# Two more blocks of the down projection by Strassen, gelu tiles moved into the weight memory, and a new order in the last group of a GeGLU kernel

## The chip, the cores and the metric

The kernel runs on one core of one Trainium2 chip. The metric is device time in microseconds (us), as the median of several executions. Each was compared with executions of the kernel before on the same chip, in the same rounds. The engines are named as in the profile: PE is TensorE (matmuls), PEld its weight loads, DVE VectorE, ACT ScalarE, POOL GpSimd, SP SyncE.

## The reference

```python
B, S, D, F = 1, 2048, 1024, 3584          # all bf16

def reference(x, w_gate, w_up, w_down):
    return (_gelu(x @ w_gate) * (x @ w_up)) @ w_down
```

## The kernel before

The tokens are worked off in two halves (h), each in two stages. The up stage makes hT = gelu(gate) * up, two blocks of 128 of F at a time. The down stage multiplies hT (28 blocks of 128 along F) by w_down, in two groups (grp) of 512 tokens. In both stages PE is relieved by Strassen's scheme: seven products (m1 to m7) instead of eight, at the price of sums of the operands, made by DVE, POOL and ACT in fp32 (t1 to t4 are sums of w_down, s1 to s4 sums of hT; a22 and b22 are copies). A "row" below is one tile of such a sum: 128 by 512 elements of w_down, 128 by 256 of hT. In down, 20 of the 28 blocks go this way (NS = 10 pairs of blocks). The other 8 are multiplied plainly, in NKK = 4 steps of 2 blocks.

Each engine takes its instructions strictly in program order: the helpers `dve`, `pool`, `act` chain them.

```python
def t_down(name, i0, i1):                  # sums of w_down, rows i0..i1 of 512
    ...
    if name in ("t2", "t4"):               # made earlier, read back from DRAM
        sp(nc.sync.dma_start(out=t.bitcast(F32), in_=src))
    elif name == "b22":
        act(nc.scalar.copy(out=t, in_=b(1, 1)))
    else:                                  # t1 and t3: on VectorE
        dve(nc.vector.tensor_tensor(out=t, in0=in0, in1=in1, op=ALU.subtract))

def s_down(hT, grp, name, i0, i1):         # sums of hT
    ...
    if name in ("s1", "s3"):
        pool(nc.gpsimd.tensor_tensor(out=t, in0=in0, in1=in1, op=op))
    else:                                  # s2 and s4
        dve(nc.vector.tensor_tensor(out=t, in0=in0, in1=in1, op=op))

def next_group():
    for i in range(0, NS, 2):
        s_down(hT, 1, "s1", i, i + 2)
    for i in range(0, NS, 2):
        s_down(hT, 1, "s3", i, i + 2)

def next_t(name, step):
    return [lambda i=i: t_down(name, i, i + step) for i in range(0, NS, step)]

then0 = {                                  # what group 0 queues behind its products
    "m5": next_t("t3", 5),
    "m4": next_t("t3", 5) + next_t("t1", 5) + [next_group],
}
```

After m4, a group runs its plain steps and evicts its eight PSUM banks. In program order this stands behind what `then0["m4"]` queued:

```python
on_act = b % 2 == (1 if last_grp else 0)
if on_act:
    act(nc.scalar.copy(out=dst, in_=banks[b][:]))
else:
    dve(nc.vector.tensor_copy(out=dst, in_=banks[b][:]))
```

So DVE makes the next group's t3 and t1 first and evicts banks 1, 3, 5 and 7 afterwards. The next group's m1 writes banks 0 and 1.

## Time and profile before

The median was 552.27 us.

| | before |
|---|---|
| PE busy | 541.3 of 550.5 us (98%) |
| DVE busy, whole span | 293.3 us (53%) |
| DVE busy in group 0 of the first half | 40.1 of 45.7 us |
| longest wait of PE | 0.9 us, in the start-up |
| pace of the up stage | 12.60 us a pair of blocks |

How to read it: PE is the bound, so another engine costs something only where PE waits for it. The average of DVE says nothing on that. Its 88% in group 0 does. The lines themselves stand in the prediction. One more from the list of transfers, since it answers to a later one: the last write of the output was the only one of these issued by ACT (size of each, and median us from issue to landing).

```profile
out_dram<-o_sb SPq DMA_DIRECT2D x7, 128.0 KB, 1.8
out_dram<-o_sb ACTq DMA_DIRECT2D x1, 128.0 KB, 2.6
```

### The profile page before, as it was taken

Reading aid. Unit: us, or ns where it says so; the run is one execution under the profiler, and the core shown is the slowest. Engines: PE = TensorE matmul, PEld = TensorE weight load, DVE = VectorE, ACT = ScalarE, POOL = GpSimd, SP = SyncE. Lnnn points to the kernel's source line nnn. Section 1 sums busy time; section 2 is a strip of 40 time slices with the busy share of each in tenths; the row PEclk is TensorE's granted clock in tenths of the full one; section 3 lists DMA queues with packets and bytes.
Section 4 is the critical chain, followed back from the end, with each engine's and each line's share of the span. In section 5 each row is a group of like instructions: output and inputs, shape, how many; then the busy total and the mean of one; then the engine's idle time right before and its main releaser. Section 6 shows DMA issues by size and latency. Waiting matters only on the chain.

```text
span 550.5 us, 7066 instructions
## 1 busy us (share of the span) xinstructions
PE 541.3 (98%) x2396; PEld 361.8 (66%) x2441; DVE 293.3 (53%) x355; ACT 245.1 (45%) x426; POOL 320.2 (58%) x248
## 2 busy tenths in 40 slices
PE   8999999999999999999999999999999999999996
PEld 3456777776777667467567767776677775765662
DVE  1714566655665896823644444444444449695402
ACT  2435545555555315117155555555555551502331
POOL 0487777777666804900598766777767763095000
PEclk9999999999999999999999999999999999999999
DMA  9642364462628789589932240405040527617803
GB/s 272 187 140 89 98 210 160 146 219 87 229 79 296 271 279 194 163 287 270 339 119 84 70 144 8 154 0 155 0 154 28 202 83 260 231 38 231 314 29 115
DMA packets 67363, 88.54 MB, mean 161 GB/s; under 512 B 15616, under 2 KB 46336, under 8 KB 67328
## 3 DMA queue, kind: packets, MB, share of 16 engines
q1 hardware_dynamic: 66640, 87.44, 49.4%
q10 hardware_dynamic: 688, 0.66, 0.4%
q8 instruction: 20, 0.33, 0.3%
q14 instruction: 15, 0.12, 0.1%
HBM read 75.50 MB, written 9.44 MB: 154 GB/s over the span
## 4 chain that ended last, share of the span: by engine, by line
PE 96%; DMA 2%; issue 0%; ACT 0%; ACTq 0%
PE bank L366 59%; PE bank L568 32%; PE bank L234 5%; DMA w_mem<-in_w_up_dram 1%; DMA wd_sb<-in_w_down_dram 1%; PE bank L288 0%; ACT o_sb L705 0%; ACTq L157 0%
## 5 line engine op out<-in xcount | busy, mean ns | idle before, releaser
L366 PE MATMUL bank<-t_mem,s_mem 128*128 128x512 f32 x1040 | 255.2, 399 | 0.0
L366 PEld LDWEIGHTS bank<-t_mem,s_mem 128*128 128x128 f32 x1040 | 195.4, 188 | 45.3
L340 POOL TENSOR_TENSOR s_mem<-w_mem 128x512 fp32r<-128x512 bf16 x104 | 125.1, 1222 | 129.1 <-PE bank L366 77.4
L389 DVE TENSOR_TENSOR bank<-bank,m 128x512 f32<-128x512 f32 x104 | 72.8, 700 | 103.3 <-ACT bank L409 91.6
L249 DVE TENSOR_TENSOR hT<-g_sb,bank 128x512 bf16<-128x512 f32 x112 | 76.8, 687 | 65.0 <-ACT g_sb L244 31.2
L244 ACT ACTIVATE g_sb<-bank 128x512 f32<-128x512 f32 x112 | 66.6, 597 | 87.4 <-DVE bank L389 49.9
L366 PE MATMUL bank<-xT,w_mem 128*128 128x512 bf16 x392 | 97.7, 380 | 1.3
L545 POOL TENSOR_TENSOR s_mem<-hT 128x512 fp32r<-128x512 bf16 (+1 forms) x32 | 67.5, 2140 | 53.2 <-PE bank L568 44.7
L568 PE MATMUL bank<-t_mem,s_mem 128*128 128x512 f32 x400 | 96.2, 397 | 0.1
L568 PEld LDWEIGHTS bank<-t_mem,s_mem 128*128 128x128 f32 x400 | 74.8, 188 | 18.1 <-issue 0.9
L568 PEld LDWEIGHTS <-hT 128*128 128x128 bf16 x416 | 39.5, 98 | 50.0 <-issue 4.4
L366 PEld LDWEIGHTS <-w_mem 128*128 128x128 bf16 x416 | 36.7, 98 | 50.5 <-issue 13.3
L495 DVE TENSOR_TENSOR t_mem<-w_mem 128x1024 fp32r<-128x1024 bf16 (+2 forms) x28 | 61.3, 2232 | 5.4 <-ACT s_mem L536 5.0
L340 POOL TENSOR_TENSOR s_mem<-s_mem,w_mem 128x512 fp32r<-128x512 f32 x52 | 61.1, 1194 | 0.0
L340 POOL TENSOR_TENSOR s_mem<-w_mem,s_mem 128x512 fp32r<-128x512 bf16 x52 | 60.0, 1173 | 0.0
L568 PE MATMUL bank<-wd_sb,hT 128*128 128x512 bf16 x244 | 55.1, 379 | 1.2 <-DMA wd_sb<-in_w_down_dram 0.4
L353 ACT CAST s_mem<-w_mem 128x512 fp32r<-128x512 bf16 x52 | 31.9, 615 | 34.0 <-PE bank L366 29.2
L404 ACT COPY m<-bank 128x512 f32<-128x512 f32 x52 | 30.6, 588 | 17.7 <-PE bank L366 17.7
L409 ACT COPY bank<-bank 128x512 f32<-128x512 f32 x52 | 29.6, 570 | 17.0 <-PE bank L366 17.0
L400 ACT COPY bank<-bank 128x512 f32<-128x512 f32 x52 | 29.6, 570 | 14.2 <-PE bank L366 14.2
L568 PE MATMUL bank<-w_mem,hT 128*128 128x512 bf16 x154 | 35.6, 379 | 0.3
L705 ACT CAST o_sb<-bank 128x512 bf16<-128x512 f32 x16 | 9.4, 586 | 56.6 <-PE bank L568 56.6
(31 smaller groups left out, 196.2 us busy)
## 6 DMA issues: line engine op xcount, KB each, us to landing
t_mem<-t_dram SPq DMA_DIRECT2D x40, 512.0 KB, 5.1
w_mem<-in_w_gate_dram SPq DMA_DIRECT2D x11, 1024.0 KB, 5.5
w_mem<-in_w_up_dram SPq DMA_DIRECT2D x11, 1024.0 KB, 7.8
w_mem<-in_w_down_dram SPq DMA_DIRECT2D x10, 1024.0 KB, 7.9
wd_sb<-in_w_down_dram SPq DMA_DIRECT2D x16, 512.0 KB, 3.7
wd_sb<-in_w_down_dram SPq DMA_DIRECT2D x20, 256.0 KB, 7.0
t_dram<-o_sb SPq DMA_DIRECT2D x20, 256.0 KB, 2.0
out_dram<-o_sb SPq DMA_DIRECT2D x12, 256.0 KB, 2.4
```

The costliest lines, as they stand in the source:

```text
L244: act(nc.scalar.activation(out=g_sb[:], in_=ps[:], func=ACT.Gelu_apprx_tanh))
L249: nc.vector.tensor_tensor(out=hT[:, fc, tb * TB : (tb + 1) * TB], in0=g_sb[:], in1=ps[:], op=ALU.mult,)
L340: pool(nc.gpsimd.tensor_tensor(out=t, in0=in0, in1=in1, op=op))
L353: act(nc.scalar.copy(out=t, in_=a(1, 1)))
L366: nc.tensor.matmul(banks[bank][:], lhsT=lhs[:, c, :], rhs=rhs[:, c, :], start=start and c == 0, stop=c == KH - 1, skip_group_check=True,)
L389: nc.vector.tensor_tensor(out=banks[dst][:], in0=banks[src][:], in1=m5[j][:], op=ALU.add)
L400: act(nc.scalar.copy(out=banks[QB[j]][:], in_=banks[PB[j]][:]))
L404: act(nc.scalar.copy(out=m5[j][:], in_=banks[VB[j]][:]))
L409: act(nc.scalar.copy(out=banks[RB[j]][:], in_=banks[QB[j]][:]))
L495: dve(nc.vector.tensor_tensor(out=t, in0=in0, in1=in1, op=ALU.subtract))
L545: pool(nc.gpsimd.tensor_tensor(out=t, in0=in0, in1=in1, op=op))
L568: nc.tensor.matmul(banks[bank][:], lhsT=lhs, rhs=rhs, start=start, stop=stop, skip_group_check=True,)
```

## The change

The intent: one more pair of blocks by Strassen (NS = 11) saves PE two matmuls a group. To make room in SBUF, the gelu tiles get no pool of their own any more: they lie in a part of the shared weight memory that is free during the up stage. With three plain steps left, all three plain tiles fit their buffers, and the last group can finish bank by bank. The diff is cut: left out are larger t_mem and s_mem, the new addresses and times of the loads of w_down and of the plain tiles, the sums of the first half's t2 and t4 made one pair earlier, and pieces that end at NS where NS is odd.

```diff
-    NS = 10
+    NS = 11
...
-    g_pool = ctx.enter_context(tc.tile_pool(name="g", bufs=4))
...
     def gelu(ps):
-        g_sb = g_pool.tile([P, TB], F32, name="g_sb")
+        e0 = 4 * CH + (g_ctr[0] % 4) * 2 * TB
+        g_sb = w_mem[:, e0 : e0 + 2 * TB].bitcast(F32)
...
     def t_down(name, i0, i1):
-        if i0 < K2A < i1:
+        for cut in (16 - NS, 8):           # rows of w_down now lie in three places
+            if i0 < cut < i1:
+                t_down(name, i0, cut)
+                t_down(name, cut, i1)
+                return
...
         if last_grp:
-            steps[-2:] = [
-                [(NKK - 2, b) for b in VB + QB[:1]]
-                + [(NKK - 1, b) for b in PB + VB + QB[:1]]
-                + [(kk, b) for b in QB[1:] + RB for kk in (NKK - 2, NKK - 1)]
-            ]
+            steps = [[(kk, b) for b in OB for kk in range(NKK) if (kk, b) not in early]]
...                                        # the last write: SyncE instead of ScalarE
-                    if b == OB[-1]:
-                        nc.scalar.dma_start(...)
+                    sp(nc.sync.dma_start(...))
...                                        # last pair of the up stage
                     "m7": [
-                        lambda: s_down(hT, 0, "s1", 8, 10),
-                        lambda: s_down(hT, 0, "s3", 0, 2),
+                        lambda: s_down(hT, 0, "s1", 8, 11),
+                        lambda: s_down(hT, 0, "s3", 0, 1),
                         lambda: t_down("t1", 0, 2),
                         lambda: t_down("t1", 2, 4),
                     ],
                     "m3": [
-                        lambda: s_down(hT, 0, "s3", 2, 6),
+                        lambda: s_down(hT, 0, "s3", 1, 5),
                         lambda: t_down("t1", 4, 6),
                     ],
...                                        # "m4": s3 in 5..8 and 8..11, t1 in 6..8 and 8..11
```

With NS = 11, `next_t(..., 5)` and the cuts make four pieces of each t: 5, 3, 2 and 1 rows. Before it was three: 2, 3 and 5.

More of the change, by code (lines that the diff above doesn't have):

```diff
@@ L71 @@
     NWD = NH * NGRP * NKK
-    K2A = 12 - NS
     assert NTB == 2 and KF % 4 == 0 and NDN == 2 and TSB == 4 and NGRP == 2
-    assert (KF // FPG) % 2 == 1 and NS == 10
+    assert (KF // FPG) % 2 == 1 and NS == 11
     xv = x2.rearrange("t (ko ki) -> t ko ki", ki=P)
@@ L94 @@
     )
-    t_mem = shared_pool.tile([P, 5 * KH * TB], F32R, name="t_mem")
-    s_mem = shared_pool.tile([P, 10 * KH * P], F32R, name="s_mem")
-    w_mem = shared_pool.tile([P, 4 * KD * FG + 4 * KD * P], BF16, name="w_mem")
+    t_mem = shared_pool.tile([P, max(5 * KH * TB, 2 * NS * DN)], F32R, name="t_mem")
+    s_mem = shared_pool.tile([P, max(10 * KH * P, 4 * NS * P)], F32R, name="s_mem")
+    CH = KD * FG
+    w_mem = shared_pool.tile([P, 4 * CH + (2 * NS - 16) * D], BF16, name="w_mem")
     t_dram = dram_pool.tile([P, 2, NS, DN], F32, name="t_dram")
@@ L138, in pe @@
         return on("pe", inst)
-    CH = KD * FG
     xs0 = w_mem[:, 4 * CH : 4 * CH + TSB * D].rearrange("p (a b) -> p a b", b=D)
@@ L240, in mm_gu @@
         )
+    g_ctr = [0]
     def gelu(ps):
-        g_sb = g_pool.tile([P, TB], F32, name="g_sb")
-        act(nc.scalar.activation(out=g_sb[:], in_=ps[:], func=ACT.Gelu_apprx_tanh))
+        e0 = 4 * CH + (g_ctr[0] % 4) * 2 * TB
+        g_ctr[0] += 1
+        g_sb = w_mem[:, e0 : e0 + 2 * TB].bitcast(F32)
+        act(nc.scalar.activation(out=g_sb, in_=ps[:], func=ACT.Gelu_apprx_tanh))
         return g_sb
@@ L250, in mult @@
                 out=hT[:, fc, tb * TB : (tb + 1) * TB],
-                in0=g_sb[:],
+                in0=g_sb,
                 in1=ps[:],
@@ L453, in wd_rows @@
     def wd_rows(k0, k1):
-        e0 = 2 * CH + k0 * D if k1 <= NS + K2A else (k0 - NS - K2A) * D
+        assert k0 // 8 == (k1 - 1) // 8 or k0 >= 16
+        e0 = (2 * CH, 0, 4 * CH)[min(k0 // 8, 2)] + (k0 - 8 * min(k0 // 8, 2)) * D
         return w_mem[:, e0 : e0 + (k1 - k0) * D].rearrange("p (a b) -> p a b", b=D)
@@ L476, in t_down @@
     def t_down(name, i0, i1):
-        if i0 < K2A < i1:
-            t_down(name, i0, K2A)
-            t_down(name, K2A, i1)
-            return
+        for cut in (16 - NS, 8):
[3 more added lines that the diff above has]
+                return
         n = 0 if name in ("t1", "t2", "t4") else 1
@@ L610, in two, with g @@
         def two(f):
-            return lambda i: f(i - 1, i + 1) if i % 2 == 1 else None
+            def g(i):
+                if i % 2 == 1 or i == NS - 1:
+                    f(i - i % 2, i + 1)
+            return g
         def to_s2_t2(i0, i1):
@@ L629, in down_group @@
         base = (h * NGRP + grp) * NKK
-        load_wd_to(base + 3)
         product("m1", PB, h_block(0, 0), wd_block(0, 0), True)
@@ L638, in down_group @@
             act(nc.scalar.copy(out=m5[u][:], in_=banks[VB[u]][:]))
+        load_wd_to(base + 3)
         product("m2", PB, h_block(0, 1), wd_block(1, 0))
@@ L654, in down_group @@
         for i in range(0, NS, 2):
-            s_down(hT, grp, "a22", i, i + 2)
+            s_down(hT, grp, "a22", i, min(i + 2, NS))
         where = {}
@@ L708, in down_group @@
                 if last_grp:
-                    if b == OB[-1]:
-                        nc.scalar.dma_start(
-                            out=out2[r0 : r0 + P, c0 : c0 + DN], in_=dst
-                        )
-                    else:
-                        sp(
-                            nc.sync.dma_start(
-                                out=out2[r0 : r0 + P, c0 : c0 + DN], in_=dst
-                            )
-                        )
+                    sp(
+                        nc.sync.dma_start(out=out2[r0 : r0 + P, c0 : c0 + DN], in_=dst)
+                    )
                 elif whole:
@@ L742 @@
             first_pair = PPG
+            stage_load(0)
         for pair in range(first_pair, NPAIR):
@@ L751 @@
                 i = pair - first_pair
+                if i + 1 < NS:
+                    then["m2"] = [lambda i=i: stage_load(i + 1)]
                 if i < NS:
-                    then["m2"] = [lambda i=i: stage_load(i)]
-                if 1 <= i <= NS:
-                    then["m4"] = [lambda i=i: stage_sums(i - 1)]
+                    then["m4"] = [lambda i=i: stage_sums(i)]
             if pair == NPAIR - PPG:
-                for k0 in range(0, NS + K2A, 4):
+                for k0 in range(0, 8, 4):
                     load_wd_rows(k0, k0 + 4)
@@ L764 @@
                     "m2": [
-                        lambda: load_wd_rows(NS + K2A, NS + K2A + 4),
-                        lambda: load_wd_rows(NS + K2A + 4, 2 * NS),
-                        lambda h=h: load_wd_to(h * NGRP * NKK + 3),
+                        lambda: load_wd_rows(8, 12),
+                        lambda: load_wd_rows(12, 16),
                     ],
                     "m7": [
-                        lambda: s_down(hT, 0, "s1", 8, 10),
-                        lambda: s_down(hT, 0, "s3", 0, 2),
+                        lambda: s_down(hT, 0, "s1", 8, 11),
+                        lambda: s_down(hT, 0, "s3", 0, 1),
                         lambda: t_down("t1", 0, 2),
@@ L779 @@
                     "m4": [
-                        lambda: s_down(hT, 0, "s3", 6, 10),
+                        lambda: load_wd_rows(16, 19),
+                        lambda: load_wd_rows(19, 22),
+                        lambda: s_down(hT, 0, "s3", 5, 8),
+                        lambda: s_down(hT, 0, "s3", 8, 11),
                         lambda: t_down("t1", 6, 8),
-                        lambda: t_down("t1", 8, 10),
+                        lambda: t_down("t1", 8, 11),
                     ],
@@ L790, in next_group @@
             for i in range(0, NS, 2):
-                s_down(hT, 1, "s1", i, i + 2)
+                s_down(hT, 1, "s1", i, min(i + 2, NS))
             for i in range(0, NS, 2):
-                s_down(hT, 1, "s3", i, i + 2)
+                s_down(hT, 1, "s3", i, min(i + 2, NS))
         def next_t(name, step):
-            return [lambda i=i: t_down(name, i, i + step) for i in range(0, NS, step)]
+            return [
+                lambda i=i: t_down(name, i, min(i + step, NS))
+                for i in range(0, NS, step)
+            ]
         then0 = {
```

## The prediction

> **What bounds the kernel now.** I read the page first (busy shares, slices, chain), then the stretches of the four groups of the down projection, then the timeline engine by engine where one group hands over to the next.
>
> ```profile
> PE 541.3 (98%) x2396; PEld 361.8 (66%) x2441; DVE 293.3 (53%) x355; ACT 245.1 (45%) x426; POOL 320.2 (58%) x248
> ...
> DVE  1714566655665896823644444444444449695402
> ...
> POOL 0487777777666804900598766777767763095000
> ...
> PE bank L366 59%; PE bank L568 32%; PE bank L234 5%; DMA w_mem<-in_w_up_dram 1%; DMA wd_sb<-in_w_down_dram 1%; PE bank L288 0%; ACT o_sb L705 0%; ACTq L157 0%
> ```
>
> TensorE (PE) is the bound: 98% busy, and 96% of the chain that ended last is matmuls. Other engines matter only where they make PE wait. The slices show where that could be: VectorE is at 8 or 9 tenths at slices 13, 14 and 16 (and again near 33 to 35), GpSimd too. Those are the first group of down in each half of the tokens. By stretch (PE, PEld, DVE, ACT, POOL busy), group 0 and group 1 of the first half:
>
> ```profile
> 187.10:232.80 45.70, 45.39 (x200) 28.54 (x205) 40.11 (x32) 13.16 (x25) 23.33 (x10) 1.00 0.81 234
> 232.80:278.70 45.90, 45.23 (x202) 28.71 (x205) 20.58 (x22) 16.70 (x29) 13.96 (x11) 1.00 0.92 286
> ```
>
> Group 0 keeps VectorE busy 40.1 of 45.7 us. The average of 53% hides an engine with 12% of slack just where the change adds work to it. The timeline of that group's end, VectorE and then GpSimd:
>
> ```profile
> 213.65 1.23 DVE L495 TENSOR_TENSOR t_mem<-w_mem 128x1024 fp32r<-128x1024 bf16 x1 [2.52 <-ACT s_mem L536]
> 215.03 14.61 DVE L495 TENSOR_TENSOR t_mem<-w_mem 128x1536 fp32r<-128x1536 bf16 x5 [0.16 <-PE bank L568]
> 230.43 0.69 DVE L707 CAST o_sb<-bank 128x512 bf16<-128x512 f32 x1 [0.79 <-PE bank L568]
> ```
>
> ```profile
> 213.69 21.41 POOL L545 TENSOR_TENSOR s_mem<-hT 128x512 fp32r<-128x512 bf16 x10 [22.37 <-PE bank L568]
> ```
>
> VectorE makes t3 and t1 of the next group (20 rows of 512, in pieces of 2, 3 and 5 rows) until 229.64 and evicts its first bank at 230.43, 0.79 us after. That 0.79 us is all the slack there is. Its queue is in program order and these sums stand ahead of the evictions.
>
> **What the Trainium skill says.** "SBUF — State Buffer", section "Who interferes with whom": VectorE and GpSimd share a port pair, as an exclusive lock, taken for a whole instruction. The trace agrees, in strict alternation. A 5-row sum took 2809 ns while GpSimd was idle (at 201.0) and 3783 ns beside it (at 217.4); a GpSimd sum took 1152 ns once VectorE had finished (230.6 to 232.8) and up to 3732 ns beside it. The difference for VectorE is one GpSimd instruction, about 1.0 us, whatever the piece's size: **the cost is per instruction**. Evictions (0.69) and gelu products (0.68) read a PSUM bank and show no such addition. "TensorE: Matmul & The Clock Gate", section "What's actually happening": the clock is halved after an idle window of about 3.4 us, the windows running freely. Before, PE never waits over 0.9 us and the granted clock is 1.00 throughout, so this trace does not test it. "DMA: Bandwidth & Descriptors", Specifications: some 358 GB/s from HBM for a core; the trace has 2 us stretches of up to 406 GB/s (188 to 190), so I use about 375.
>
> **The change, part by part.**
>
> *Matmuls.* The eleventh pair of blocks replaces 16 plain matmuls per group by 14 of Strassen: 4 bf16 and 10 fp32r. Their pace: one pair of the up stage repeats every 12.60 us (the chain: 12.55 + 0.05) with 40 fp32r and 16 bf16; m2, m6 and m7 of group 0 (20 bf16, 40 fp32r) run from 196.41 to 209.86, 13.45 us. The difference of 4 bf16 and 0.85 us gives 0.2125 us for a bf16 matmul and then 0.230 for an fp32r one. Saved: 12 x 0.2125 - 10 x 0.230 = 0.25 us a group, **1.0 us in all**. The arithmetic gain is this small.
>
> *Three plain tiles instead of four.* They fit the three buffers, so the wait on the fourth at the end of the first half (0.43 us on PE at 275.2) goes: **-0.4 us**.
>
> *gelu tiles in the shared memory.* Still four slots, reused after four gelus as before. The rows 16 to 21 of w_down that later use this place must wait for the last gelu products (until about 192 us), 1.5 MB, some 4 us at 375 GB/s; m2 reads row 16 after about 200. Hidden: **0**. Rows 8 to 11 now come in late, with a load issued at about 181 that lands some 6 to 8 us on; m1 needs row 8 at 190.5. Hidden too. t2 (2.75 MB) and the plain tiles land before m6 and the early plain matmuls.
>
> *End.* The last group's banks follow one another; the last eviction (0.59) and write are as exposed as before: **0**.
>
> *The start of group 0.* t1 is being made while m1 and m5 run.
>
> ```profile
> 185.05 4.29 DVE L495 TENSOR_TENSOR t_mem<-w_mem 128x1024 fp32r<-128x1024 bf16 x2
> 189.27 0.68 DVE L249 TENSOR_TENSOR hT<-g_sb,bank 128x512 bf16<-128x512 f32 x1
> 189.87 2.54 DVE L495 TENSOR_TENSOR t_mem<-w_mem 128x1024 fp32r<-128x1024 bf16 x1
> 192.33 0.67 DVE L249 TENSOR_TENSOR hT<-g_sb,bank 128x512 bf16<-128x512 f32 x1
> 192.93 2.35 DVE L495 TENSOR_TENSOR t_mem<-w_mem 128x1024 fp32r<-128x1024 bf16 x2
> ```
>
> PE already loses about 0.5 us here (m1 and m5 take 9.34 us against 20 x 0.2125 + 20 x 0.230 = 8.85; the waits of PEld name this line with 0.6). Now GpSimd's s1 piece has 3 rows (and must wait for both m7 products, to 183.7), and its s3 comes as 1, 4, 3 and 3 rows instead of 2, 4 and 4. Alternating by the lock, with 0.55 us a row on either engine: GpSimd to 185.3, t1(0-2) to 186.5, GpSimd 187.1, t1(2-4) 188.2, GpSimd 190.3, t1(4-6) 191.5, GpSimd 193.1, t1(6-8) 194.3, GpSimd 195.9, t1(8-11) 197.6. m5 wants row 8 at 187.07 + 22 x 0.2125 + 16 x 0.230 = 195.4. Stall 2.1 us instead of 0.5: **+1.6 us a half**.
>
> *The end of group 0.* Counted from the start of m3. Before: m3, m4 and the 52 plain matmuls left take 40 x 0.230 + 52 x 0.2125 = 20.25 us, so m3 starts at 232.81 - 20.25 = 212.56 and the sums end 17.1 later. After: 44 x 0.230 + 40 x 0.2125 = 18.6 us, so PE arrives 1.6 us sooner. VectorE meanwhile has 22 rows in 8 instructions (5, 3, 2, 1, twice) for 20 in 6. Without the lock a set takes 2.75 + 1.68 + 1.13 + 0.60 = 6.16 us, both 12.3. The first piece needs five rows free, not two, so GpSimd has taken the lock twice before, to 3.4. Between the eight lie seven GpSimd instructions, six of 1.03 and one half-size, 6.75. End: 3.4 + 12.3 + 6.75 = 22.45 after m3 began; the eviction of bank 1 (0.69 and a semaphore) makes it 23.2. The next group's m1 writes bank 1 with its second matmul, at 18.6 + 0.2. **PE stalls 4.4 us**, once a half. The other evictions follow at 0.69 each and hold nothing up.
>
> Sum per half: group 0 -0.25 + 1.6 + 4.4, group 1 -0.25, so +5.5; twice +11.0; less 0.4: **+10.6, to 562.9 us**.
>
> **Rivals.** (1) *The gain comes through*: 552.3 - 1.4, about 551. For it: PE is the chain, and nothing else is over 58% busy. Against it: the slack of 0.79 us in front of the first eviction, with 5.3 us added to VectorE's end and 1.6 taken from PE's. (2) *The clock drops in the new gap*: 4.4 us can hold a whole idle window of 3.4 us or not, by where the window falls. An estimate from that page: about one in three a gap, and each loses some 1.7 to 3 us of half clock, so 565 to 568 in some executions. (3) *The transfers become the wait*: w_down rows held back by gelu products would stop PE in m2 or m6, one or two us a half. The DMA share is about 1.0 from 184 to 200, which speaks for it; against it are the 6 to 8 us between landing and use worked out above. (4) *Only the first stall or only part of the second comes*: if GpSimd's pieces slip, the lock alternates less often, each skipped turn gives back 1 us, and the time is 555 to 560.
>
> **Range and chances.** 2% over 552.28 is 563.3, so the sum lies a hair under the line. Of the runs that go as worked out, I give half to each side, the clock pushing up; about a fifth I keep for a wait smaller than thought. Slower by over 2%: 0.43, within 0.56, faster 0.01. Range 555 to 568, time 563.0.
>
> **What would show it.** Right: group 0 about 51.5 us long in each half, group 1 about 45.5; PE idle for over 4 us at the second matmul of group 1's m1, ended by the VectorE eviction of a bank; before it the t_mem sums as one run of 8 instructions of some 19 us; a wait of PE on t_mem of about 2 us in m5. The DVE line of the up stage unchanged. Wrong: evictions on VectorE close behind their banks as before, or a PE wait on w_mem or wd_sb. A granted clock under 1.00 would be rival 2. What would break the prediction: alternation that does not hold with smaller pieces, or evictions that overtake the sums.

## The result, and the profile after

564.14 us, the median of 4 executions (564.01 to 565.45), against 552.27: a ratio of 1.0219, with a 95% interval of 1.0201 to 1.0237, so slower by just over 2%. Ratios here and below are the mean time of one kernel's executions over that of the other's in the same rounds, so not quite the ratio of the medians quoted.

First the waits of PE in the kernel after (what it waited for: us in total, times, longest). DVE did not appear in this list before, but for a start-up wait of 0.2 us (on PEld, the weight loads, t_mem had 0.6 us in two waits):

```profile
PE bank L572 <- DVE o_sb L711: 7.2, 2, 3.6
PE bank L572 <- DVE t_mem L499: 2.7, 4, 0.8
```

The first is an eviction, the second the sums of w_down. The timeline of DVE at the end of group 0 in the first half:

```profile
217.66 19.44 DVE L499 TENSOR_TENSOR t_mem<-w_mem 128x2560 fp32r<-128x2560 bf16 x8 [3.02 <-ACT s_mem L540]
237.02 2.47 DVE L711 CAST o_sb<-bank 128x512 bf16<-128x512 f32 x4
```

and of PE at the same place, where group 1 begins:

```profile
225.34 8.58 PE L572 MATMUL bank<-wd_sb,hT 128*128 128x512 bf16 x39
233.76 0.38 PE L572 MATMUL bank<-w_mem,hT 128*128 128x512 bf16 x1
237.75 6.16 PE L572 MATMUL bank<-w_mem,hT 128*128 128x512 bf16 x20 [3.61 <-DVE o_sb L711]
243.56 5.36 PE L572 MATMUL bank<-t_mem,s_mem 128*128 128x512 f32 x22
248.76 4.92 PE L572 MATMUL bank<-w_mem,hT 128*128 128x512 bf16 x21
253.33 10.39 PE L572 MATMUL bank<-t_mem,s_mem 128*128 128x512 f32 x44
```

m1's first matmul goes into bank 0. Its second stands until 237.75, when DVE has finished eight sums and evicted bank 1 at last. Before, the sums were one instruction and a run of five, and the eviction followed its bank with time to spare.

The other stall is in m5 of group 0, which now waits twice for the sums of w_down. Before, PE ran it in one piece:

```profile
191.21 5.36 PE L568 MATMUL bank<-t_mem,s_mem 128*128 128x512 f32 x20
```

After:

```profile
191.44 3.12 PE L572 MATMUL bank<-t_mem,s_mem 128*128 128x512 f32 x12
195.36 1.20 PE L572 MATMUL bank<-t_mem,s_mem 128*128 128x512 f32 x4 [0.80 <-DVE t_mem L499]
197.12 1.63 PE L572 MATMUL bank<-t_mem,s_mem 128*128 128x512 f32 x6 [0.57 <-DVE t_mem L499]
```

The chain of the kernel after now runs through DVE here (start, length, what):

```profile
223.87 0.12 DVE t_mem L499
...
225.98 11.12 DVE t_mem L499 x5
237.09 0.61 DVE o_sb L711
...
237.75 3.57 PE bank L572 x9
```

The starts in the timeline of PE (first column) show something more: m1 has 22 matmuls, as has m2 of the same group (a matmul record is missing here and there), but m2 takes 4.57 us (248.76 to 253.33) and m1 takes 9.80 (233.76 to 243.56). The gap accounts for 3.77 of the 5.23 us of difference. The rest is the clock. Stretches of the kernel after, gap and m1 of the first half, then of the second half (length, busy time of PE, PEld, DVE, ACT and POOL; then the granted clock, the share of DMA, GB/s):

```profile
233.80:237.70 3.90, 0.34 (x2) 0.06 (x1) 3.90 (x4) 0.31 (x1) 3.90 (x3) 0.95 0.28 109
237.70:243.60 5.90, 5.80 (x21) 2.40 (x21) 1.79 (x3) 0.00 (x0) 2.14 (x3) 0.74 0.37 136
507.20:511.20 4.00, 0.40 (x2) 0.10 (x1) 4.00 (x4) 0.38 (x1) 4.00 (x3) 0.90 0.17 66
511.20:517.50 6.30, 6.07 (x15) 2.32 (x16) 1.76 (x3) 0.00 (x0) 2.10 (x3) 0.52 0.34 127
```

The granted clock falls to 0.74 and 0.52 in the stretches after the gaps. In the trace it is at half from 237.3 on for 3.4 us, and from 510.4 on for 6.8 us.

The whole difference of the two profiled executions, stage by stage (differences of the starts of stages):

| stage | change, us |
|---|---|
| group 0 without the gap, both halves | +1.15 and +1.14 |
| gap at m1 of group 1 | +3.77 twice |
| m1 at the lower clock (9.80 and 11.29 us less the gap, against 4.57) | +1.46 and +2.95 |
| rest of group 1 | -0.91 and -0.34 |
| start of the last matmul to the end (4.58 before, 3.67 after) | -0.91 |
| start-up and up stages | -0.2 |
| sum (spans: 562.34 - 550.48) | +11.9 |

### The profile page after: what moved, and what is told of

Read it like the earlier page. It is cut to its first block, busy times and chain, and to the rows that moved or that the text cites. A ratio compares the mean times of both kernels' runs of the same rounds, so it can differ in the third digit from the quotient of the medians.

```text
span 562.3 us, 7155 instructions
## 1 busy us (share of the span) xinstructions
PE 544.6 (97%) x2390; PEld 365.8 (65%) x2433; DVE 308.6 (55%) x374; ACT 248.1 (44%) x434; POOL 328.1 (58%) x254
## 4 chain that ended last, share of the span: by engine, by line
PE 87%; DVE 8%; issue 3%; DMA 1%; ACT 0%; ACTq 0%; DVEq 0%
PE bank L368 57%; PE bank L572 25%; DVE t_mem L499 7%; PE bank L232 5%; DMA w_mem<-in_w_up_dram 1%; DVE hT L251 1%; DVE bank L391 0%; DVE o_sb L711 0%; PE bank L290 0%; ACT o_sb L709 0%; ACTq L155 0%; DVEq L499 0%; DVEq L251 0%
## 5 line engine op out<-in xcount | busy, mean ns | idle before, releaser
L368 PE MATMUL bank<-t_mem,s_mem 128*128 128x512 f32 x1040 | 255.2, 399 | 0.0
L368 PEld LDWEIGHTS bank<-t_mem,s_mem 128*128 128x128 f32 x1040 | 195.4, 188 | 45.3
L251 DVE TENSOR_TENSOR hT<-w_mem,bank 128x512 bf16<-128x512 f32 x112 | 76.7, 687 | 64.9 <-ACT w_mem L246 31.1
L572 PE MATMUL bank<-t_mem,s_mem 128*128 128x512 f32 x440 | 105.5, 396 | 2.7 <-DVE t_mem L499 2.7
L549 POOL TENSOR_TENSOR s_mem<-hT 128x512 fp32r<-128x512 bf16 (+3 forms) x38 | 75.5, 2016 | 55.1 <-PE bank L572 46.6
L246 ACT ACTIVATE w_mem<-bank 128x512 f32<-128x512 f32 x112 | 66.6, 596 | 87.4 <-DVE bank L391 49.9
L572 PEld LDWEIGHTS bank<-t_mem,s_mem 128*128 128x128 f32 x440 | 82.3, 188 | 22.5 <-DVE t_mem L499 2.4
L368 PE MATMUL bank<-xT,w_mem 128*128 128x512 bf16 x391 | 95.2, 380 | 1.5
L499 DVE TENSOR_TENSOR t_mem<-w_mem 128x1024 fp32r<-128x1024 bf16 (+3 forms) x36 | 73.5, 2098 | 6.0 <-ACT s_mem L540 6.0
L572 PEld LDWEIGHTS <-hT 128*128 128x128 bf16 x368 | 36.0, 101 | 54.6 <-issue 17.2
L572 PE MATMUL bank<-w_mem,hT 128*128 128x512 bf16 x169 | 43.6, 409 | 7.8 <-DVE o_sb L711 7.2
L572 PE MATMUL bank<-wd_sb,hT 128*128 128x512 bf16 x184 | 41.4, 379 | 0.5
```

The costliest lines, as they stand in the source:

```text
L246: act(nc.scalar.activation(out=g_sb, in_=ps[:], func=ACT.Gelu_apprx_tanh))
L251: nc.vector.tensor_tensor(out=hT[:, fc, tb * TB : (tb + 1) * TB], in0=g_sb, in1=ps[:], op=ALU.mult,)
L368: nc.tensor.matmul(banks[bank][:], lhsT=lhs[:, c, :], rhs=rhs[:, c, :], start=start and c == 0, stop=c == KH - 1, skip_group_check=True,)
L572: nc.tensor.matmul(banks[bank][:], lhsT=lhs, rhs=rhs, start=start, stop=stop, skip_group_check=True,)
```

## The experiments

The theory: DVE and POOL lock each other out for whole instructions. More and smaller DVE sums therefore end later, and the eviction behind them stops PE. The gap lets the clock drop. The rivals: the engines share bandwidth, so that elements count; or bank 1 waits for something else; or m1 is slow for another reason.

One observation for all runs: the executions of every kernel spread over some 1.5 us by their start-up. In the profiles of e2, e3 and e5, m1 of the first group began at 188.3 to 188.5, in those of e7 and e8 at 189.1 and 189.5 (0.5 us of that is a wait of their own). In those of before, after, e1, e4, e6, e9 and e10 it began at 186.8 to 187.1. In the late ones the clock rises to full at 9.5 to 10.1 us, in the others at 3.7 to 5.4. Stages are therefore compared by their lengths, not by the end of the run. And e5 to e8 ran on another chip, where the kernel before took 553.47 us: their medians are to be compared by the ratio.

**e1: evictions of group 0 on ScalarE.**

```diff
-                on_act = b % 2 == (1 if last_grp else 0)
+                on_act = b % 2 == (1 if last_grp else 0) or grp == 0
```

> The changed kernel, with all eight evictions of the first group of each half on ScalarE. Theory (the eviction of bank 1 stands behind the sums in VectorE's queue, and the gap of 3.8 us that follows lets the TensorE clock drop): both gaps (2 x 3.77) and both drops of the clock (1.46 + 2.95 us of slow matmuls) go, so 564.1 - 11.9 = 552.2 us, granted clock 1.00, no PE wait on o_sb; the waits on t_mem at the start of the first group stay at about 2.7 us. The sums on VectorE still end at about 237. Rival (the bank waits for something else, a transfer or GpSimd): a wait of some 4 us at the same matmul with another releaser, and 560 us or more.

Measured: 552.91 us, ratio 0.9996 (0.9971 to 1.0021), granted clock 1.00. Of the two waits on DVE only that for t_mem is left:

```profile
PE bank L572 <- DVE t_mem L499: 2.7, 4, 0.8
```

DVE's sums still took 19.44 us. This settles that the place of the eviction in DVE's queue made the gap. That the change's own saving does not show is put down to m5 of group 0, which still took 7.15 us; e9 tests it.

**e2: the same rows in fewer DVE instructions.**

```diff
-                lambda i=i: t_down(name, i, min(i + step, NS))
-                for i in range(0, NS, step)
+                lambda i=i, e=e: t_down(name, i, e)
+                for i, e in ((0, 5), (5, 8), (8, NS))
```

> The changed kernel with t3 and t1 of the next group in pieces of 5, 3 and 3 rows instead of 5, 3, 2 and 1: the same rows in 6 VectorE instructions instead of 8. Theory (the port pair is locked per instruction, VectorE and GpSimd alternate): two turns of GpSimd of 1.05 us fewer stand in between, the sums end about 2.1 us earlier, the gap shrinks from 3.8 to about 1.7 us, too short for the clock to drop: 564.1 - 4.2 - 4.4 = about 555.5 us. Rival (the two engines share bandwidth, so that the elements count): the same end, within 0.2 us, and 564 us.

Measured: 556.59 us, ratio 1.0058 (1.0029 to 1.0087). The profile has a late start (188.4), which is most of the 1.1 us above the expectation.

```profile
219.22 17.39 DVE L499 TENSOR_TENSOR t_mem<-w_mem 128x2560 fp32r<-128x2560 bf16 x6 [3.02 <-ACT s_mem L540]
```

```profile
PE bank L572 <- DVE o_sb L711: 3.1, 2, 1.6
```

17.39 instead of 19.44 us for the same elements: two instructions fewer are worth 2.05 us. The gap is 1.6 us, and no drop of the clock follows it.

**e4: the same elements in more and smaller GpSimd instructions.**

```diff
-            for i in range(0, NS, 2):
-                s_down(hT, 1, "s1", i, min(i + 2, NS))
+            for i in range(NS):
+                s_down(hT, 1, "s1", i, i + 1)          # s3 likewise
```

> The changed kernel with the next group's s1 and s3 sums on GpSimd cut into single rows: 22 instructions of about 0.6 us instead of 12 of about 1.1. Work on VectorE and its instructions unchanged. Theory (lock per instruction, strict alternation): each GpSimd turn between two VectorE sums costs 0.55 instead of 1.05 us, the VectorE sums end about 3.4 us earlier, the gap is about 0.4 us and the clock holds: 564.1 - 6.7 - 4.4 = about 553.0 us. GpSimd's own run gets longer but ends before m7 of the next group needs it. Rival (elements count, not instructions): 564 us, or slower for the added fixed costs.

Measured: 552.44 us, ratio 0.9988 (0.9965 to 1.0010). Nothing on DVE was changed, and its eight sums now take:

```profile
217.77 15.72 DVE L499 TENSOR_TENSOR t_mem<-w_mem 128x2560 fp32r<-128x2560 bf16 x8 [3.02 <-ACT s_mem L540]
```

3.7 us less than in the kernel after (19.44). The wait for the eviction is gone from the list. e2 and e4 together refute shared bandwidth: the elements were the same in both, and only the number or the size of instructions differed.

**e3: the gap filled with matmuls.**

```diff
+        if grp == 1:
+            for _ in range(16):
+                mm(PB[0], h_block(0, 0)(0, 0), wd_block(0, 0)(0), True, True)
         product("m1", PB, h_block(0, 0), wd_block(0, 0), True)
```

> The changed kernel with 16 more matmuls into bank 0 ahead of the second group's m1 in each half (their result is overwritten by m1's first matmul). They fill 16 x 0.215 = 3.4 us of the gap of 3.8 us with work. Theory (part of the loss is the clock, which drops after an idle window): the wait for the eviction ends at the same time as before, but the granted clock stays 1.00 and m1 runs at full pace: 564.1 - 4.4 = 559.7 us. Rival (m1 is slow after the gap for another reason, or the added matmuls simply cost their time): 564 us or up to 571 us.

Measured: 561.25 us, ratio 1.0143 (1.0118 to 1.0167), in a profile with a late start (188.4). The added matmuls change nothing in the result: m1's first matmul overwrites them. The wait for the eviction shrank to 0.3 us in all, and m1 kept its pace:

```profile
239.33 4.69 PE L572 MATMUL bank<-w_mem,hT 128*128 128x512 bf16 x21 [0.17 <-DVE o_sb L714]
243.68 5.39 PE L572 MATMUL bank<-t_mem,s_mem 128*128 128x512 f32 x22
```

From the start of group 0's m1 to group 1's m5 it is 55.23 us here (188.45 to 243.68) against 56.69 after (186.87 to 243.56). The 1.46 us are exactly what the table above puts down to the clock. The granted clock was 1.00 in the stretches of both gaps. PE's idleness, not the gap's other work, made the clock drop.

**e5: the kernel before, with only the last write on SyncE.** Edit: the branch to `nc.scalar.dma_start` taken out, as in the change.

> The kernel before with one part of the change alone: the last write of the output issued by SyncE like the others, not by ScalarE. In the profiles the last write took 2.65 us from issue to landing on ScalarE's queue before and about 1.7 us on SyncE's queue after. Theory (the queue sets it): about 0.9 us faster, 551.4 us. Rival (the shorter end of the changed kernel comes from its order of banks, which spaces the writes): no change, 552.3 us.

Measured: 553.01 us against 553.47, ratio 1.0000 (0.9981 to 1.0020). By time this is inconclusive, the spread of the start-up hides 1 us, and the profiled execution started late. By its trace, the span ends 2.62 us after the last eviction. In the kernel before that was 3.58 us, and in the ten other profiles with the last write on SyncE it was 2.66 or 2.67 us, but for e10 with 2.98. The last write itself took 1.69 us from issue to landing, 2.64 before (1.70 or 1.71 in the others, 2.05 in e10). The median of the eight writes:

```profile
out_dram<-o_sb SPq DMA_DIRECT2D x8, 128.0 KB, 1.8
```

So the queue accounts for about 0.9 us at the end, shown by the traces, not by the measured times. It is one write in one profile: ScalarE issues no other in that stretch, so whether each write of its queue is slower there is not shown.

**e6: the kernel after, with the last group's matmuls in the old order.** Edit: the old `steps[-2:]` put back, all writes on SyncE.

> The changed kernel with the last group's plain matmuls in the order of the kernel before, all writes still on SyncE. Theory (the order of the banks does not matter, the last bank's eviction and write are exposed either way): 564.1 us, same within 0.3. Rival (bank by bank hides evictions): slower by 0.5 to 1 us.

Measured: 563.65 us, ratio 1.0188 (1.0173 to 1.0203), with both gaps and both drops of the clock as after; by the 2% line it is unclear whether it is slower. The half microsecond less than 564.14 does not come from the order: from m5 of the last group to the last matmul it is 40.18 us here and 40.16 after, and 3.67 from there to the end in both. Bank by bank is worth nothing measurable.

**e7: t1 earlier and in three pieces.**

```diff
-        for cut in (16 - NS, 8):
+        for cut in (8,) if name == "t1" else (16 - NS, 8):
...
+                    "m6": [..., lambda: t_down("t1", 0, 4)],
                     "m7": [...,
-                        lambda: t_down("t1", 0, 2),
-                        lambda: t_down("t1", 2, 4),
+                        lambda: t_down("t1", 4, 8),
                     ],
-                    # t1 4..6 after m3 and 6..8 after m4: taken out
```

> The changed kernel with t1 of the first group made earlier and in three pieces (rows 0 to 4 after m6 of the last pair, 4 to 8 after m7, 8 to 11 at the end) instead of six on VectorE. Theory (m5 waits for t1 because its pieces alternate with GpSimd's s3 under the lock): the waits of PE on t_mem, 2 x 1.95 us lost in m5, go: 564.1 - 3.5 to 3.9 = about 560.4 us; the gap at the second group's m1 and the clock drop stay. Rival (m5 waits for s1 on GpSimd or for the loads of rows 8 to 11): m5 still about 7 us long, 564 us.

Measured: 561.50 us, ratio 1.0146 (1.0129 to 1.0164): 1.1 us above the expectation, on the slower chip. m5 was clean (5.23 us), and group 0 up to the gap became 1.9 us shorter in each half, so the theory on t1 holds. The clock drop of the second half lasted 3.4 us here instead of 6.8, worth some 1.3 us. But a new wait of PE came up in the up stage:

```profile
PE bank L368 <- DVE bank L391: 1.1, 2, 0.5
```

The early piece of t1 stood, locked out by POOL, ahead of DVE's additions of m5 to the banks, and the last product of the pair waited for those. The mend moved part of the wait on.

**e8: e1 and e7 together.**

> The changed kernel with both mends: evictions of the first group of each half on ScalarE, and t1 early in three pieces. If the two stalls and the clock are the whole loss and independent: 564.1 - 11.9 - 3.7 = 548.5 us, that is 3.8 us faster than the kernel before: 1.0 us of matmuls saved, 0.4 us of the wait for a plain tile, 1.0 us of the last write, and 1.2 us of m5's wait in the kernel before. Rival (a stall removed in one place comes back in the next stage): 550 us or more.

Measured: 551.03 us, ratio 0.9956 (0.9942 to 0.9969). Faster than before, but by 2.4 us instead of 3.8. The wait of e7 is still there (1.1 us in the list), and it costs more than the list says: the up stage of the second half takes 177.22 us, 0.83 more than after. Three of the six executions took 551.5 to 552.1 us and three 550.5; the profiled one is of the slower kind and started late.

**e9: e1, with t1 only after m7 and POOL's s3 in pieces of two rows.**

```diff
...                                        # e1's line, and e7's on the cuts of t1
                     "m7": [...,
-                        lambda: t_down("t1", 0, 2),
-                        lambda: t_down("t1", 2, 4),
+                        lambda: t_down("t1", 0, 4),
                     ],
                     "m3": [
-                        lambda: s_down(hT, 0, "s3", 1, 5),
-                        lambda: t_down("t1", 4, 6),
+                        lambda: s_down(hT, 0, "s3", 1, 3),
+                        lambda: s_down(hT, 0, "s3", 3, 5),
+                        lambda: t_down("t1", 4, 8),
                     ],
                     # "m4": s3 in 5..7, 7..9 and 9..11, t1 in 8..11
```

> The version with both mends again, but t1's first piece only after m7 (so that VectorE adds the m5 term to the banks in time, which e7 and e8 delayed: PE waited 0.5 us twice) and GpSimd's s3 in pieces of two rows, so that VectorE's turns come sooner. Theory: the new waits on bank go, m5 waits at most 0.3 us. By the stages of the changed kernel's profile: 564.1 - 7.5 - 4.4 - 3.3 = 548.9 us in executions whose clock rises early (by 5 us), 1.4 more where it rises at 10 us, as seen in half of the profiles: median about 549.5, 0.7% under the kernel before. Rival (each mend moves the wait on): 551 us as for e8.

Measured: **548.76 us**, ratio 0.9940 (0.9927 to 0.9954), the fastest version. PE waits for no other engine after the start-up. m5 of the first group starts at 191.44 and m2 at 196.66:

```profile
191.44 5.39 PE L572 MATMUL bank<-t_mem,s_mem 128*128 128x512 f32 x22
196.66 4.92 PE L572 MATMUL bank<-w_mem,hT 128*128 128x512 bf16 x22
```

**e10: the kernel before with the same mends** (evictions of group 0 on ScalarE, t1 in 4, 4 and 2 rows, s3 in pieces of two rows, last write on SyncE).

> The kernel before (20 of 28 blocks by Strassen) with the same mends: first group's evictions on ScalarE, t1 in three pieces, s3 in pieces of two rows, last write on SyncE. It shows what two more blocks by Strassen are worth where neither kernel stalls. Theory: 8 matmuls fewer and one wait on a plain tile fewer are worth 1.0 + 0.4 us, so this one is 1.4 us slower than e9, about 550.9 us. Rival (the mends need the changed kernel, or the matmuls' saving is lost): equal to e9, or no better than the kernel before, 552.3.

Measured: 550.21 us, ratio 0.9964 (0.9951 to 0.9977): 1.45 us slower than e9 on the same chip in the same rounds. Where nothing stalls, a group takes 44.98 us with NS = 11 (e9, 186.86 to 231.84) and 45.31 us with NS = 10 (e10, 186.90 to 232.21). The four groups differ by 0.31 to 0.34 us, 1.3 us in all: the whole worth of the added Strassen blocks. The forecast of 1.4 was met in part by luck: its 0.4 for the wait on a plain tile is not in it, since e10 has no such wait either (that load took 4.2 us to land, 5.5 in the kernel before), and e10's profile lost 0.3 us at the end, where its last write took 2.05 us.

## Why the prediction was right or wrong

The predicted time was 563.0 us, the measured one 564.14, inside the range. The chance was put slightly to the wrong side of the 2% line. The mechanism of both stalls was the predicted one. That the sum came within 1.2 us is partly luck, since its errors cancelled: 4.4 us of clock were left out, and the gaps were put 1.3 too long, the end 0.9 and the matmuls 0.3 too dear.

- **The gap**: predicted 4.4 us a half, measured 3.77. Counted from the recorded start of m3 (214.92), DVE's sums ended 22.2 us later (predicted 22.45), and PE stood at m1's second matmul 19.06 us later (predicted 18.8). The alternation held in all eight steps; e2 and e4 confirm that the price is one POOL instruction for each DVE instruction.
- **The start of group 0**: predicted +1.6 us a half. m5 took 7.15 us against 5.22 without waits (e9), so it lost 1.93. Before, it lost 0.43 (5.20, against 4.77 in e10). That is +1.5. I had overlooked that the new cut at row 5 also splits t1's rows 4 to 6 into two instructions, and that s1's last piece need not wait until 183.7 (it started at 183.03).
- **The clock**: this step failed. It stood among the rivals, at "about one in three a gap". The drop came in both gaps of the profile, and the granted clock was 0.99 in all four executions. The size was about right (1.7 to 3 us each was forecast, 1.46 and 2.95 measured), the chance was not: it asked for a whole window of 3.4 us without work inside the gap. In the traces of after, e6 and e7, six gaps of 3.8 us, the clock dropped each time, although the 3.41 us before the drop held 0.06 to 0.63 us of matmuls. In the gaps of 1.6 us (e2) it did not drop. The two drops cost 4.41 us in the profile, of which e3 took back 4.34. With it in the sum, the verdict would have been slower by over 2%.
- **The end**: "as exposed as before: 0" was wrong by 0.9 us. The list of transfers of the kernel before already showed 2.6 us for ScalarE's write and 1.8 for SyncE's. I had priced the eviction and not the queue.
- **The matmuls**: 0.25 us a group predicted, 0.33 measured (e9 and e10). The pace of the two kinds was worked out from whole stages, with the changes from one product to the next in them; that this makes the difference is argued, not tested.
- **The plain tile**: a wait of 0.43 us before, none on wd_sb after, as predicted. That the third tile's fit removed it is not shown: e10, with four plain steps, has none either.
- **The gelu tiles**: predicted 0. The up stage of the second half took 176.41 us before (278.68 to 455.09) and 176.39 after (283.95 to 460.34).
- **The rivals**: transfers did not become the wait (no wait of PE on w_mem or wd_sb after the start-up). The reading that the gain comes through failed, for the reason given against it. Rival 3 quotes "6 to 8 us between landing and use", but the working above it has that as the time from issue to landing, and a margin of 1.5 to 3.5 us before use. In the record rows 8 to 11 landed at 186.49, in time. Rival 1's "nothing else is over 58% busy" leaves out PEld with 66%, which is TensorE's own.

What stays open: what sets how long the clock stays down after such a gap. No run varied this alone. The six drops in the traces of after, e6 and e7 suggest that it is how much of the gap lies behind the drop: with 0, 0, 0.42 and 0.68 us the clock was back after 3.4 us, with 0.81 and 0.93 us after 6.8.

## What to carry to other kernels

Before adding work to an engine that is not the bound, look for the stage in which it is full and for what stands behind the new work in its queue: here an eviction that the bound engine needed at once. Where VectorE and GpSimd make sums side by side, count instructions rather than elements. Of 19.44 us, fewer and larger ones on the engine that others wait for gave 2.05 back (e2), and smaller ones on the other engine 3.7 (e4), without touching a sum. A gap in the matmuls may cost more than its length: 3.77 us of waiting cost 5.2 and 6.7.

## What the Trainium skill lacked or had wrong

- "SBUF — State Buffer", section "Who interferes with whom": the exclusive lock is right. The page lacks the consequence for two streams side by side: strict alternation, so each VectorE sum pays for one GpSimd instruction. Eight sums took 19.44 us beside pieces of two rows and 15.72 beside pieces of one row.
- "TensorE: Matmul & The Clock Gate", section "What's actually happening", has the clock halved after an idle window of about 3.4 us, with the windows running freely. The trace agrees in length: 3.41 and 6.83 us at half. The page lacks how much work a window may hold and still count as idle: here drops came after 3.41 us with up to 0.63 us of matmuls in them, in six of six gaps of 3.8 us, and in neither gap of 1.6 us (e2). It also lacks how idle a window may be and still bring the clock back: see the six drops above.
- "DMA: Bandwidth & Descriptors", section "Issuing engines are not separate DMA queues", treats SyncE's and ScalarE's queues alike. Here the one last write of 128 KB on ScalarE's queue took 2.64 us from issue to landing; on SyncE's it took 1.69 to 1.71 in ten profiles and 2.05 in one. The profile with ScalarE ended 3.58 us after its last eviction, the others 2.62 to 2.98. It is a single write, so this is a hint, not a rule.
